# Gated mix of two attentions: half of the value units moved from the lead into the main steps, output units cut in two, differences reduced by relu in the lead

## The chip, the cores and the metric

The kernel runs on one core of a Trainium2 chip. The metric is device time in microseconds from the first to the last instruction of a launch, as the median of several runs. One execution was also recorded by the hardware profiler; all views below are of that execution. Engines: PE (matmul), DVE (vector), ACT (activation), POOL (GpSimd) and SP, which here only issues DMAs. Each engine works through its own instructions in order; semaphores order them against each other.

## The reference

Two attentions over the same x of 2048 positions and 576 features, 32 heads of 18 each. A has a key and a value for each head, B one key and one value for all heads. A sigmoid gate for each position mixes the two results:

```python
g = _sigmoid((x * gate_w).sum(-1, keepdims=True))
a = _A_ref(x, A_wqkv, A_wo)
b = _B_ref(x, B_wq, B_wk, B_wv, B_wo)
return g * a + (1 - g) * b
```

with, in each, softmax(q k^T / sqrt(18)) v for every head and an output matrix of 576 x 576. All is float32; the kernel splits numbers into a high and a low part to keep the precision.

## The kernel before, in words

**Heads and steps.** The 64 heads (`NU`; first the 32 of B, u < `H`, then the 32 of A) are worked off one after the other. A head has 16 steps, so there are 1024 (`NSTEP`). A step of the softmax takes 128 keys against all 2048 queries: four score matmuls of 512 columns (`step_scores`, L548), each followed by an exponential on ACT (L555) that writes a `pt` tile, and the output product (`step_pv`, L561), which multiplies the four `pt` tiles of an earlier step with the values and accumulates in the bank `acc`.

**The maxima.** The exponentials need the row maximum of each query. It is found `LEAD` = 22 steps ahead by `step_max`: for 128 queries, matmuls against the keys in four chunks of 512 (L511), each into a bank `pm`, and a reduction on DVE (L520). In the main steps one chunk of every second step is not reduced by itself. Instead the operation "x" multiplies with the difference of the keys of chunk 1 and chunk 0, ACT writes its relu to the tile `xb` (L514), and one custom DVE instruction (L517) adds `xb` to chunk 0 and takes the maximum, which covers both chunks. `max_rows` finishes a head's maxima; they go through DRAM into two extra rows of `qs`.

**Order.** The order of the work is written by hand, for two steps at a time (a pair, A and B), as strings at L789 to L795. "s" is a score, "m" a maximum (a capital M uses the other half of the PE rows), "x" the difference matmul for the next pair; P, Q, p, f, h, H are output products, whole (P, Q) or half; U takes one piece of the list `todo`; V projects values. The string of a plain pair and that of a pair with a unit:

```python
PLAIN = "sA0 mA2 sA1 mA0 sA2 mA3 P sA3 mB0 sB0 mB1 sB1 mB2 h sB2 mB3 sB3 x H"
UNIT = "sA0 mA2 sA1 mA0 sA2 mA3 P sA3 mB0 sB0 mB1 sB1 mB2 U sB2 mB3 sB3 x Q"
```

END stands for the last pair of a head (step number divisible by 16), AFTER for the one behind it. A score and the maximum next to it use different rows of the PE array and run at the same time.

**Banks.** The eight PSUM banks are three for scores (`ps_s`), four for maxima and for everything else that needs a bank for a short time (`ps_m`), and `acc`. A pool hands its banks out in turn; a matmul waits until the last reader of its bank is done.

**Stages.** First the projections of q and k for all heads (L240). Then the lead, steps -22 to -1: eleven pairs of maxima with no scores yet (`LEADS`), and between them 32 value units (`project_v`, L289): for one block of 128 positions and one half of A's heads 14 matmuls of 288 columns into a score bank, a copy on ACT (L292) and a store to DRAM, from where groups of four heads are loaded again later. Then the main steps. In steps 522 to 848 the first output segment (`out_proj` with `first`) adds 32 units of twelve matmuls (L677) and a copy on ACT (L683), in pairs with the string UNIT, one piece each (`at_ends`); the second segment follows in steps 942 to 1007 with a unit in nearly every pair, evicted by DVE. From step 1002 there are no more maxima (ALONE), and a short tail adds the last head.

Of the kernel before, what the change touches and what calls it, by code (L numbers as in the profile page):

```python
# [8 lines left out]
F32 = mybir.dt.float32  # L9
# [29 lines left out]


def q_row(u):
    return ROW_Q + DH * u if u < H else ROW_Q + DH * H + 2 * DH * (u - H)
# [7 lines left out]
def gated_mix_kernel(ctx: ExitStack, tc: tile.TileContext, xT, wall, wv, wo, out):  # L50
# [109 lines left out]
    def turn_mask():  # L160
        pt = ps_m.tile([P, 512], F32, name="pm")
# [31 lines left out]
    def balance(g):  # L193
# [9 lines left out]
        yield  # L203
        pt = ps_m.tile([P, 512], F32, name="pm")
        nc.tensor.transpose(pt[0:2, 0:P], r, ident)
# [5 lines left out]
        yield  # L211
        pb = ps_m.tile([P, 512], F32, name="pm")
        nc.tensor.matmul(pb[:, 0:2], two, dg, start=True, stop=True)
# [58 lines left out]
    def shared_v(c):  # L272
        st = ST.pop(c)
        pv = ps_m.tile([P, 512], F32, name="pm")
# [117 lines left out]
    vwp = ph1.enter_context(tc.tile_pool(name="vwp", bufs=1, side="right"))  # L392
    VS = [None, None]

# [3 lines left out]
    def project_rest():  # L398
        bal = None
        for n in range(12, len(JOBS)):  # L400
            mt, c = JOBS[n]
            if c == 0 and mt + 1 < MT:
                WP.append(prep_w(W[mt + 1]))
            project(n)
            for m in range(*AT.get(n, (0, 0))):
                measure_a(m, W[m])
            if n == 13:
                bal = balance(2)
            if n in (13, 14):
                next(bal)  # L410
            if n == 15:
                run(bal)
            if c == 0:
                if mt == 4:
                    load_k(ksb, ROW_KB, nc.gpsimd)
                    load_kd(kdb, ROW_KB, nc.gpsimd)
                if mt == 5:
                    load_q(0, nc.gpsimd)
                if mt in (6, 7):
                    load_q(mt - 5, nc.gpsimd)  # L420
                if mt in (7, 10):
                    hf = (mt - 7) // 3
# [45 lines left out]
    def open_ph2():  # L468
# [6 lines left out]
        L["kds"] = [p2.tile([P, 512], F16, name="kda"), kdb]  # L475
        L["oacc"] = p2.tile([P, 16, D], F32, name="oacc")
        for t in L["ks"][:2]:
# [13 lines left out]
    def v_of(u, kt):  # L491
# [3 lines left out]
        return VG[g][:, kt, 19 * i:19 * i + 19]  # L495

    MX = {}

    def step_max(u, i, c, low=False):

# [10 lines left out]
        nc.tensor.matmul(pm, qs[u % 3][b:b + 54, i * P:(i + 1) * P], k, start=True, stop=True)  # L511
# [135 lines left out]
    def out_proj(t0, rows, first=False):  # L647

        nt = len(rows)
        oacc = L["oacc"]  # L650
        O = {}
# [14 lines left out]
        for q in range(8):  # L666
# [3 lines left out]
            for s2 in range(2):  # L670
                st_ = 2 * q + s2
                for hf in range(2):
                    fp = ps_m.tile([P, 512], F32, name="pm")
                    n = 0
                    for a, b in PRODS:
                        for t, r in enumerate(rows):
                            nc.tensor.matmul(fp[:, 0:288], o[b][:r, t, s2 * P:(s2 + 1) * P],  # L677
                                             w[a][:r, t, 288 * hf:288 * hf + 288],
# [25 lines left out]
    def last_out():  # L704
# [6 lines left out]
        for j in range(4):  # L711
# [3 lines left out]
            dma(stk[36:54, cs], ol[32 * j:32 * j + 18, :])  # L715
        pt = ps_m.tile([P, 512], F32, name="pm")
        for c in range(4):
# [7 lines left out]
        for st_ in range(16):  # L725
            for hf in range(2):
                ps = ps_m.tile([P, 512], F32, name="pm")
                nc.tensor.matmul(ps[:, 0:288], stk[0:54, st_ * P:st_ * P + P],
# [41 lines left out]
    for t0, rows, Ta, Tb, Tc in SEG:  # L770
        when(Ta, lambda t0=t0, rows=rows: slow.append(prep_wo(t0, rows)))
        when(Tb - 4, lambda t0=t0, rows=rows: (todo.append(out_proj(t0, rows, first=t0 == 0)), pull(1)))
    when(980, lambda: slow.append(prep_last()))


    at_ends = list(range(528, 849, 16)) + list(range(522, 843, 32))
    assert len(at_ends) == 32

    def due(T, t0, t1, n):
        if t0 == SEG[0][3]:  # L780
            return at_ends.count(T)
# [12 lines left out]
    ALONE = "sA0 sA1 P U sA2 sA3 U sB0 sB1 h U sB2 sB3 H U"  # L794
    LEADS = "V.A mA0 MA1 mA2 MA3 V.B mB0 MB1 mB2 MB3"  # L795
    order = None
    for T in range(-LEAD, NSTEP + 2, 2):
# [8 lines left out]
        units = sum(due(t, Tb, Tc, 32) for t in (T, T + 1) for _, _, _, Tb, Tc in SEG)  # L806
        order = LEADS if T < 0 else FIRST if T == 0 else ALONE if alone else UNIT if units else \
            END if T % 16 == 0 else AFTER if order is END else PLAIN
        for op in order.split():
            k, second, c = op[0], op[1:2] == "B", op[2:]  # L810
            if k == "V":
                while len(vunits) > 32 * (-T - 1 - (c == "B")) // LEAD:
                    project_v(*vunits[0], WV[vunits[0][1]])
# [4 lines left out]
            elif k in "mM":  # L818
                step_max(*divmod(M + second, 16), int(c), k == "M")
            elif k == "s":  # L820
# [57 lines left out]
```

## Time and profile before

| what | value |
|---|---|
| median of 3 runs | 2726.04 us (2725.89 to 2726.05) |
| the profiled execution | 2726.16 us, span 2724.3 us |
| PE, DVE, ACT busy | 99%, 89%, 88% of the span |
| projections, before the lead | to 224.7 us |
| the lead | 224.7 us to 307.2 us (start of the first exponential) |
| the main steps, relu of step 0 to relu of step 998 | 312.6 us to 2637.7 us |

How to read the rows that follow. A row of the timeline or of the chain begins with its start and its duration in us, then engine, line, operation and tiles (output, arrow, inputs), shape, and the number of instructions that are merged in the row; in square brackets stands the idle time of the engine before it and who ended it. A row of the table by stage begins with the stage (from:to), then its length, then busy time and number of instructions for each engine named in its first row, then the granted PE clock, the share of the DMA engines and GB/s. Matmul records of neighbours overlap, so the distance between starts tells more than the durations. In the rows `pm` is a maxima bank, `ps` a score bank; `kdb` and `kda` as inputs mark the difference matmul x.

### The profile page before, as it was taken

Reading aid. Unit: us, or ns where it says so; the run is one execution under the profiler, and the core shown is the slowest. Engines: PE = TensorE matmul, PEld = TensorE weight load, DVE = VectorE, ACT = ScalarE, POOL = GpSimd, SP = SyncE. Lnnn points to the kernel's source line nnn. Section 1 sums busy time; section 2 is a strip of 40 time slices with the busy share of each in tenths; the row PEclk is TensorE's granted clock in tenths of the full one; section 3 lists DMA queues with packets and bytes.
Section 4 is the critical chain, followed back from the end, with each engine's and each line's share of the span. In section 5 each row is a group of like instructions: output and inputs, shape, how many; then the busy total and the mean of one; then the engine's idle time right before and its main releaser. Section 6 shows DMA issues by size and latency. Waiting matters only on the chain.

```text
span 2724.3 us, 57935 instructions
## 1 busy us (share of the span) xinstructions
PE 2689.0 (99%) x22210; PEld 957.2 (35%) x22210; DVE 2421.9 (89%) x4589; ACT 2389.5 (88%) x4809; POOL 285.7 (10%) x531
## 2 busy tenths in 40 slices
PE   8999999999999999999999999999999999999999
PEld 6767522222222222222222333333333332223444
DVE  6335899999999999999999999999999999998865
ACT  4332599999999999999999999999999999998875
POOL 3641000001000200110110001000100021001000
PEclk9999999999999999999999999999999999999998
DMA  6322100002001100110132113112221112122312
GB/s 188 114 97 85 38 16 19 20 22 59 27 18 32 45 26 17 45 43 20 32 72 80 41 49 97 40 41 57 72 66 48 47 58 64 39 68 85 89 36 95
DMA packets 127089, 150.36 MB, mean 55 GB/s; under 512 B 55339, under 2 KB 94411, under 8 KB 125614
## 3 DMA queue, kind: packets, MB, share of 16 engines
q1 hardware_dynamic: 113628, 121.86, 15.8%
q0 software_dynamic: 7968, 19.23, 2.1%
q10 hardware_dynamic: 5216, 5.57, 0.6%
q8 instruction: 174, 2.85, 0.4%
q14 instruction: 103, 0.84, 0.1%
HBM read 90.89 MB, written 46.45 MB: 50 GB/s over the span
## 4 chain that ended last, share of the span: by engine, by line
ACT 50%; PE 40%; DVE 6%; DMA 2%; issue 1%; SPq 1%; POOL 0%; DVEq 0%; ACTq 0%; POOLq 0%
ACT pt L555 45%; PE acc L561 13%; PE ps L548 11%; ACT xb L514 6%; PE pm L677 4%; PE ps L240 4%; PE pm L240 4%; DVE mx L520 3%; PE ps L289 3%; PE pm L511 1%; SPq L56 1%; DMA R<-r_d 1%; DVE oe L571 1%; DVE junk L517 1%; DVE oacc L731 0%
## 5 line engine op out<-in xcount | busy, mean ns | idle before, releaser
L555 ACT ACTIVATE pt<-ps 128x512 f32<-128x512 f32 x4052 | 2093.2, 637 | 67.8 <-PE pm L511 59.8
L520 DVE TENSOR_REDUCE mx<-pm 128x1 f32<-128x512 f32 x3096 | 1941.4, 683 | 93.6 <-PE pm L511 52.8
L548 PE MATMUL ps<-qs,ksb 56*128 56x512 f16 x2688 | 818.4, 380 | 10.7
L511 PE MATMUL pm<-ksb,qs 54*128 54x512 f16 x2364 | 742.2, 383 | 2.2 <-DVE mx L520 1.1
L561 PE MATMUL acc<-pt,vb 128*19 128x512 f32 (+1 forms) x6136 | 592.2, 458 | 1.9
L561 PE MATMUL acc<-pt,vg 128*19 128x256 f32 (+1 forms) x5664 | 579.5, 481 | 2.3 <-DVE oe L571 0.5
L511 PEld LDWEIGHTS <-qs 54*128 54x128 f16 x4096 | 332.2, 93 | 245.6 <-issue 196.7
L548 PE MATMUL ps<-qs,ksa 56*128 56x512 f16 x1364 | 404.3, 379 | 4.8 <-ACT pt L555 1.3
L548 PEld LDWEIGHTS <-ksb 56*128 56x128 f16 x2688 | 175.0, 94 | 622.1 <-issue 575.8
L511 PE MATMUL pm<-ksa,qs 54*128 54x512 f16 x1232 | 384.8, 382 | 0.5 <-ACT xb L514 0.2
L517 DVE CUSTOM_DVE_ANT_0 junk<-pm,xb 128x512 bf16<-128x512 f32 x500 | 340.6, 681 | 0.0
L514 ACT ACTIVATE xb<-pm 128x512 f32<-128x512 f32 x500 | 316.6, 633 | 0.0
L548 PEld LDWEIGHTS <-ksa 56*128 56x128 f16 x1408 | 89.3, 94 | 328.8 <-issue 298.1
L530 POOL TENSOR_SCALAR mt<-mt 128x32 f32<-128x32 f32 x64 | 18.6, 290 | 1612.0 <-DVE mt L528 1612.0
L561 PEld LDWEIGHTS acc<-pt,vb 128*19 128x19 f32 x6136 | 104.1, 96 | 223.5 <-issue 206.4
L561 PEld LDWEIGHTS acc<-pt,vg 128*19 128x19 f32 x5664 | 96.1, 97 | 222.8 <-issue 204.9
L511 PE MATMUL pm<-kdb,qs 54*128 54x512 f16 x372 | 141.5, 380 | 0.0
L248 ACT ACTIVATE ph<-ps,tv 128x512 f16<-128x512 f32 x29 | 19.8, 686 | 67.3 <-PE ps L240 43.2
L292 ACT ACTIVATE vst<-ps 128x288 f32<-128x288 f32 x32 | 13.2, 412 | 67.4 <-PE ps L289 67.4
L571 DVE COPY oe<-acc 128x512 f32<-128x512 f32 x63 | 43.6, 692 | 30.0 <-PE acc L561 27.9
L248 ACT ACTIVATE ph<-pm,tv 128x512 f16<-128x512 f32 x27 | 18.4, 686 | 54.5 <-PE pm L240 40.6
L254 DVE SCALAR_TENSOR_TENSOR pl<-pm,tv,ph 128x512 f16<-128x512 f32 x27 | 20.1, 749 | 48.8 <-ACT ph L248 38.7
(151 smaller groups left out, 1518.6 us busy)
## 6 DMA issues: line engine op xcount, KB each, us to landing
qs<-qkh SPq DMA_DIRECT2D x244, 72.0 KB
qs<-qkl SPq DMA_DIRECT2D x122, 72.0 KB
onh<-oh SPq DMA_DIRECT2D x32, 256.0 KB
onl<-ol SPq DMA_DIRECT2D x32, 256.0 KB
oih<-onh SPq DMA_DIRECT2D x16, 512.0 KB
oil<-onl SPq DMA_DIRECT2D x16, 512.0 KB
ot<-oe SPq DMA_DIRECT2D x220, 36.0 KB
R<-r_d SPq DMA_DIRECT2D x55, 144.0 KB
```

Of the source, the lines that this page charges most:

```text
L240: nc.tensor.matmul(fp[:, a0:b0], w[a][:kr, k, :], X[b][:kr, k, s0 + a0:s0 + b0], start=(n == 0), stop=(n == len(PROJ) - 1), skip_group_che ...
L248: nc.scalar.activation(h, fp, AF.Copy, scale=t)
L289: nc.tensor.matmul(fp[:, 0:288], X[b][:kr, k, st_ * P:(st_ + 1) * P], w[a][:kr, k, :], start=(n == 0), stop=(n == len(PROJ) - 1))
L511: nc.tensor.matmul(pm, qs[u % 3][b:b + 54, i * P:(i + 1) * P], k, start=True, stop=True)
L514: nc.scalar.activation(MX["x", u, i], pm, AF.Relu)
L517: nc.vector.tensor_tensor_reduce(junk, pm, MX.pop(("x", u, i)), 1.0, -3e38, op0=OP.add, op1=OP.max, accum_out=MX[u][:, i, c:c + 1])
L520: nc.vector.tensor_reduce(MX[u][:, i, c:c + 1], pm, axis=AX.X, op=OP.max)
L548: nc.tensor.matmul(ps, kst(u)[b:b + 56, i * P:(i + 1) * P], qs[u % 3][b:b + 56, c * 512:(c + 1) * 512], start=True, stop=True)
L555: nc.scalar.activation(pt, ps, AF.Exp, scale=SCALE / LIFT ** 2)
L561: nc.tensor.matmul(acc[32 * j:32 * j + 19, a:b], v_of(u, i), PT[u, i, j][:, a:b], start=(i == 0 and a == 0), stop=(i == 15), skip_group_ch ...
L571: nc.vector.tensor_copy(oe, acc)
L677: nc.tensor.matmul(fp[:, 0:288], o[b][:r, t, s2 * P:(s2 + 1) * P], w[a][:r, t, 288 * hf:288 * hf + 288], start=(n == 0), stop=(n == 3 * nt ...
```

## The change

Banks: `ps_m` shrinks from four to three; the fourth becomes a pool of its own, `ps_x`, whose bank `side()` hands out. Value units, output units, the transposes of the setup and every fourth of the banks asked for through `four()` use it. `four()` serves the maxima of the lead and the tail, the plain `ps_m` the maxima of the main steps.

Values: only the first half of A's heads (16 units) is projected in the lead. The other 16 units are made by the new `value_units` among steps 16 to 434, each in two bursts of seven matmuls in the place of U: positions and weights are loaded again from DRAM and split on GpSimd, two units share double buffers, and the tiles live where the output accumulator and the first output weights are later. Pairs with a burst take the string UNIT instead of PLAIN, END or AFTER.

Output: the first segment's 32 units are cut in two bursts of six, 64 pieces from step 524 on (`pieces`).

Lead: its first pair reduces all eight chunks and ends with an x; the other ten replace one reduction of step A by that relu, as the main steps do, and the first main pair has one maximum less.

```diff
+VPROD = PROJ[:-1] + [("l", "h", NKT - 1, 128)]
...
-    ps_m = ctx.enter_context(tc.tile_pool(name="ps_m", bufs=4, space=PSUM))
+    ps_m = ctx.enter_context(tc.tile_pool(name="ps_m", bufs=3, space=PSUM))
+    ps_x = ctx.enter_context(tc.tile_pool(name="ps_x", bufs=1, space=PSUM))
...
+    turn = {"n": 0}
+
+    def side():
+        return ps_x.tile([P, 512], F32, name="px")
+
+    def four():
+
+        turn["n"] += 1
+        return side() if turn["n"] % 4 == 0 else ps_m.tile([P, 512], F32, name="pm")
...
-                if mt in (9, 12):
-                    hf = (mt - 9) // 3
-                    WV.append({y: vwp.tile([P, NKT, 288], F32R, name=f"vw{y}{hf}") for y in "hl"})
-                    split_w(VS[hf], WV[hf], nc.vector)
+                if mt == 9:
+                    WV.append({y: vwp.tile([P, NKT, 288], F32R, name=f"vw{y}") for y in "hl"})
+                    split_w(VS[0], WV[0], nc.vector)
...
+    def value_units():
...
+        def parts(src, st, h, l):
+            dma(st[:, 0:4, :], src[0:512, :].rearrange("(k p) m -> p k m", p=P))
+            for b in (0, 64):
+                dma(st[b:b + 64, 4, :], src[512:576, :])
+            return st, h, l
...
+        def cut(st, h, l):
+            split(st, h, l, nc.gpsimd, nc.gpsimd)
+            return {"h": h, "l": l}
...
+        for st_ in range(16):
+
+            nc.gpsimd.tensor_tensor(x["h"][64:128, 4], st[64:128, 4], x["h"][64:128, 4].bitcast(F32), op=OP.subtract)
+            if st_ < 15:
+                nxt = positions(st_ + 1)
+            yield
+            fp = side()
+            for n, (a, b, k, kr) in enumerate(VPROD):
+                if n == 7:
+                    yield
+                nc.tensor.matmul(fp[:, 0:288], x[b][:kr, k, :], w[a][:kr, k, :],
+                                 start=(n == 0), stop=(n == len(VPROD) - 1))
+            t = vs[st_ % 2]
+            nc.scalar.activation(t[:, :, 0:18], fp[:, 0:288].rearrange("p (h d) -> p h d", d=18), AF.Copy)
+            dma(v_d[st_, :, 304:608], t.rearrange("p h d -> p (h d)"))
+            if st_ < 15:
+                x = cut(*nxt)
+                st, h, l = nxt
...
-        pm = ps_m.tile([P, 512], F32, name="pm")
+        pm = four() if lead_on else ps_m.tile([P, 512], F32, name="pm")
...
-                    fp = ps_m.tile([P, 512], F32, name="pm")
+                    fp = four() if "tail" in L else side()
                     n = 0
                     for a, b in PRODS:
                         for t, r in enumerate(rows):
+                            if first and n == 6:
+                                yield
...
+    when(0, lambda: (todo.append(value_units()), pull(1)))
...
-    at_ends = list(range(528, 849, 16)) + list(range(522, 843, 32))
-    assert len(at_ends) == 32
+    pieces = [524 + 11 * i // 4 * 2 for i in range(64)]
+
+    vpieces = [0] + [16 + 27 * i // 4 * 2 for i in range(32)]
...
-    vunits = [(st_, hf) for hf in range(2) for st_ in range(16)]
+    vunits = [(st_, 0) for st_ in range(16)]
...
-    FIRST = "sA0 mA2 sA1 mA0 sA2 mA3 mA1 sA3 mB0 sB0 mB1 sB1 mB2 sB2 mB3 sB3 x"
+    FIRST = "sA0 mA2 sA1 mA0 sA2 mA3 sA3 mB0 sB0 mB1 sB1 mB2 sB2 mB3 sB3 x"
...
-    LEADS = "V.A mA0 MA1 mA2 MA3 V.B mB0 MB1 mB2 MB3"
+    LEAD0 = "V.A mA0 MA1 mA2 MA3 V.B mB0 MB1 mB2 MB3 x"
+    LEADS = "V.A mA2 MA0 mA3 V.B mB0 MB1 mB2 MB3 x"
...
+        if T >= NSTEP - 6:
+            L["tail"] = True
```

More of the change, by code (lines that the diff above doesn't have):

```diff
@@ L160, in turn_mask @@
     def turn_mask():
-        pt = ps_m.tile([P, 512], F32, name="pm")
+        pt = side()
         for g in range(4):
@@ L203, in balance @@
         yield
-        pt = ps_m.tile([P, 512], F32, name="pm")
+        pt = side()
         nc.tensor.transpose(pt[0:2, 0:P], r, ident)
@@ L211, in balance @@
         yield
-        pb = ps_m.tile([P, 512], F32, name="pm")
+        pb = side()
         nc.tensor.matmul(pb[:, 0:2], two, dg, start=True, stop=True)
@@ L273, in shared_v @@
         st = ST.pop(c)
-        pv = ps_m.tile([P, 512], F32, name="pm")
+        pv = side()
         for j in range(4):
@@ L392, in gated_mix_kernel @@
     vwp = ph1.enter_context(tc.tile_pool(name="vwp", bufs=1, side="right"))
-    VS = [None, None]
+    VS = [None]
     for b in (SB, MB):
@@ L475, in open_ph2 @@
         L["kds"] = [p2.tile([P, 512], F16, name="kda"), kdb]
-        L["oacc"] = p2.tile([P, 16, D], F32, name="oacc")
         for t in L["ks"][:2]:
@@ L495, in v_of, with place, positions, step_max @@
         return VG[g][:, kt, 19 * i:19 * i + 19]
+    def value_units():
+        rooms = {"r": (F32R, "oacc"), "w": (F32, "woh4"), "x": (F32, "wol4")}
+        used = {"r": 0, "w": 0, "x": 0}
+        room = {r: L["pool"].tile([P, 16 * D if r == "r" else 4 * D], t, name=f"room_{r}", tag=g)
+                for r, (t, g) in rooms.items()}
+        def place(r, k, m):
+            n = used[r]
+            used[r] += k * m
+            return room[r][:, n:n + k * m].rearrange("p (k m) -> p k m", m=m)
+        def parts(src, st, h, l):
[3 more added lines that the diff above has]
+            return st, h, l
+        XV = [[place(r, NKT, P) for r in "xrr"] for j in range(2)]
+        def positions(st_):
+            return parts(xT[:, P * st_:P * st_ + P], *XV[st_ % 2])
+        def cut(st, h, l):
+            split(st, h, l, nc.gpsimd, nc.gpsimd)
+            return {"h": h, "l": l}
+        nxt = positions(0)
+        w = parts(wv[:, 288:576], *[place(r, NKT, 288) for r in "wrr"])
+        vs = [place("x", 16, 19) for i in range(2)]
+        yield
+        w = cut(*w)
+        x = cut(*nxt)
+        st, h, l = nxt
+        for t in vs:
+            nc.gpsimd.memset(t, 1.0)
+        for st_ in range(16):
[13 more added lines that the diff above has]
+            if st_ < 15:
+                x = cut(*nxt)
+                st, h, l = nxt
     MX = {}
-    def step_max(u, i, c, low=False):
+    def step_max(u, i, c, low=False, lead_on=False):
         if u not in MX:
@@ L649, in out_proj @@
         nt = len(rows)
+        if first:
+            L["oacc"] = L["pool"].tile([P, 16, D], F32, name="oacc")
         oacc = L["oacc"]
@@ L676, in out_proj @@
                         for t, r in enumerate(rows):
+                            if first and n == 6:
+                                yield
                             nc.tensor.matmul(fp[:, 0:288], o[b][:r, t, s2 * P:(s2 + 1) * P],
@@ L715, in last_out @@
             dma(stk[36:54, cs], ol[32 * j:32 * j + 18, :])
-        pt = ps_m.tile([P, 512], F32, name="pm")
+        pt = four()
         for c in range(4):
@@ L726, in last_out @@
             for hf in range(2):
-                ps = ps_m.tile([P, 512], F32, name="pm")
+                ps = four()
                 nc.tensor.matmul(ps[:, 0:288], stk[0:54, st_ * P:st_ * P + P],
@@ L805, in gated_mix_kernel @@
         alone = M >= NSTEP
-        units = sum(due(t, Tb, Tc, 32) for t in (T, T + 1) for _, _, _, Tb, Tc in SEG)
-        order = LEADS if T < 0 else FIRST if T == 0 else ALONE if alone else UNIT if units else \
+        units = sum(due(t, Tb, Tc, 32) for t in (T, T + 1) for _, _, _, Tb, Tc in SEG) + vpieces.count(T)
+        order = LEAD0 if T == -LEAD else LEADS if T < 0 else FIRST if T == 0 else ALONE if alone else UNIT if units else \
             END if T % 16 == 0 else AFTER if order is END else PLAIN
@@ L818, in gated_mix_kernel @@
             elif k in "mM":
-                step_max(*divmod(M + second, 16), int(c), k == "M")
+                step_max(*divmod(M + second, 16), int(c), k == "M", T < 0)
             elif k == "s":
```

8 lines of the change are left out of this document (4 added, 4 removed).

## The prediction

> **What bounds the kernel now.** I read the busy time of each engine by stage first, then the chain of waits in the lead, then the timelines of single pairs of steps.
>
> ```profile
> span 2724.3 us, 57935 instructions
> ...
> core 0: us, PE busy (x) PEld busy (x) DVE busy (x) ACT busy (x) POOL busy (x), PEclk, DMA share, GB/s
> 224.70:307.20 82.50, 82.35 (x540) 65.13 (x540) 54.27 (x90) 14.19 (x35) 2.78 (x13) 1.00 0.20 70
> 349.40:1355.50 1006.10, 995.95 (x8964) 281.40 (x8960) 987.08 (x1881) 994.07 (x2017) 65.91 (x129) 1.00 0.11 30
> ```
>
> The stage that the change empties, the lead (224.7 to 307.2 us), has PE full and ACT nearly idle. The main stage has PE, DVE and ACT all at 98 or 99%, but a busy matmul time says little about PE there (records overlap), so the stages must be read instruction by instruction. The lead, in the chain of waits:
>
> ```profile
> 224.75 4.49 PE ps L289 x28
> 229.24 0.45 PE pm L511 x3
> 229.69 2.26 PE ps L289 x14
> 231.94 0.45 PE pm L511 x3
> ```
>
> Each value unit (14 matmuls) holds PE 2.25 us, each four maxima 0.45 us, with nothing between them. DVE waits for PE there: four reductions take 2.48 us, 0.62 each, and the next four matmuls come 2.7 us after the last at the earliest (229.24 to 231.94).
>
> ```profile
> 229.38 2.48 DVE L520 TENSOR_REDUCE mx<-pm 128x1 f32<-128x512 f32 x4 [3.07 <-PE ps L289]
> ```
>
> Now one pair of the main stage. The string PLAIN orders it: A0, A1, A2 are scores and maxima of the first step, then P, an output product, then A3 and the second step.
>
> ```profile
> 687.14 0.60 ACT L555 ACTIVATE pt<-ps 128x512 f32<-128x512 f32 x1
> ...
> 687.33 0.39 PE L511 MATMUL pm<-ksb,qs 54*128 54x512 f16 x1
> 687.55 0.38 PE L511 MATMUL pm<-ksb,qs 54*128 54x512 f16 x1
> 687.62 0.61 ACT L514 ACTIVATE xb<-pm 128x512 f32<-128x512 f32 x1
> 687.80 0.39 PE L511 MATMUL pm<-ksb,qs 54*128 54x512 f16 x1
> 688.10 4.06 ACT L555 ACTIVATE pt<-ps 128x512 f32<-128x512 f32 x8
> 688.12 1.06 PE L561 MATMUL acc<-pt,vb 128*19 128x512 f32 x8
> ...
> 689.11 0.39 PE L548 MATMUL ps<-qs,ksb 56*128 56x512 f16 x1
> ...
> 690.08 0.63 PE L561 MATMUL acc<-pt,vb 128*19 128x256 f32 x8
> 690.64 0.39 PE L548 MATMUL ps<-qs,ksb 56*128 56x512 f16 x1
> ...
> 692.03 0.61 ACT L514 ACTIVATE xb<-pm 128x512 f32<-128x512 f32 x1
> ```
>
> From relu to relu 4.41 us: nine ACT instructions, 0.48 us apart at the relu (687.62 to 688.10) and 0.49 behind it ((4.06 - 0.60) / 7). But P sits on this path as well: it starts at 688.12, and the score behind it (sA3) starts only at 689.11, 0.99 us later. ACT comes to sA3's exponential after three others, at 688.10 + 3 x 0.48 to 0.49 = 689.54 to 689.57, which is 0.43 to 0.46 us after that score's start. Where ACT stands idle and waits for this score (the next fence), the delay is 0.42. So sA3 arrives just in time, with hardly any slack. The half product h at 690.08 holds PE 0.56.
>
> **The change, part by part.**
>
> *Three banks for the maxima instead of four.* This is the largest term. The difference matmul of one pair (x) is followed by mA2, mA0 and mA3 of the next. At 687.80, when mA3 starts, x is held by its relu until 687.62 + 0.61 = 688.23, mA2 by its reduction, and mA0 by the custom instruction, which reads the relu's result. With four banks there is one left. With three there is none, and x's is the first to come free. So mA3 waits until 688.28 (an exponential's bank, released at 687.14 + 0.60 = 687.74, was taken by sA2 beside mA3 at 687.80: 0.05 to see a release), 0.48 late; P is queued behind it on PE, sA3 behind P, and ACT waits for sA3. The new loop is relu 0.61, release 0.05, mA3 to P 0.31 (687.80 to 688.12), P 0.99, sA3 to ACT 0.42, then A3, B0 to B3 up to the next relu, 5 x 0.48 = 2.40: 4.78 us where 4.41 stood. The trace has one pair where exactly this happens, because DVE was late and mA3's bank with it:
>
> ```profile
> 870.28 0.37 PE L511 MATMUL pm<-kdb,qs 54*128 54x512 f16 x1
> ...
> 871.35 0.61 ACT L514 ACTIVATE xb<-pm 128x512 f32<-128x512 f32 x1
> ...
> 872.08 0.37 PE L511 MATMUL pm<-ksb,qs 54*128 54x512 f16 x1
> 872.38 1.05 PE L561 MATMUL acc<-pt,vb 128*19 128x512 f32 x8
> ...
> 873.37 0.39 PE L548 MATMUL ps<-qs,ksb 56*128 56x512 f16 x1
> ...
> 873.79 2.56 ACT L555 ACTIVATE pt<-ps 128x512 f32<-128x512 f32 x5 [0.36 <-PE pm L511]
> ...
> 876.19 0.64 ACT L514 ACTIVATE xb<-pm 128x512 f32<-128x512 f32 x1
> ```
>
> mA3 started 0.12 us after the relu's end, ACT stood idle 0.36 us, and the pair took 4.84 us. Less 0.07 for the later start, that is my 4.78.
>
> The pair at a head's end (END) has the same chain up to A3 and then three steps to its relu: 2.38 + 1.44 = 3.82, now 3.36:
>
> ```profile
> 669.56 0.61 ACT L514 ACTIVATE xb<-pm 128x512 f32<-128x512 f32 x1
> ...
> 672.92 0.69 ACT L514 ACTIVATE xb<-pm 128x512 f32<-128x512 f32 x1
> ```
>
> How many pairs, and what they take on average now (the relus counted by stage):
>
> ```profile
> core 0: us, ACT busy (x), PEclk, DMA share, GB/s
> 349.40:1355.50 1006.10, 143.79 (x224) 1.00 0.11 30
> 1503.10:2262.80 759.70, 99.69 (x160) 1.00 0.20 56
> 2480.20:2620.00 139.80, 14.48 (x24) 1.00 0.26 79
> ```
>
> A plain pair is 1006.1 / 224 = 4.49 us, eight to a head of 16 steps. Of the eight, five are as above and lengthen by 0.33 (4.78 against 4.41 to 4.49); END adds 0.46. Of the two after END, x comes early in one, so that nothing is late (taken as 0), and in the other mA3 waits for the last maximum of the pair before: taken as 0.25, between 0 and 0.43. Sum 2.4 us for a head. Bounds: 1.6 if only the five change, 3.4 if all eight lose the 0.43 of the late pair. Steps 4 to 942 are 58.6 heads: +141 (94 to 199). The last stage (24 pairs in 139.8, 5.82 each) is bound by PE's unit of twelve matmuls in every pair; the relu is done there before mA3. +3 (0 to 7) for some 30 pairs.
>
> *The lead.* 16 units leave: 16 x 2.25 = 36 us off PE. What remains on PE is 16 x 2.25 + 22 x 0.45 = 46 us. DVE has 8 + 10 x 7 = 78 reductions at 0.62, 48 us, now the longer. The two alternate: five pairs hold two units, 5.4 us on PE; six hold one, 4.3 on DVE; 53 in all, from 48 if the banks smooth it to 58 if each unit delays DVE. The relu of the differences lies on an ACT that is 17% busy. From 82.5 to 53: -29 (-34 to -24). The second half's weight split, no longer done in the projections, lay beside a full PE: nothing.
>
> *Value units in the main stage.* Thirty-two bursts of seven matmuls, in place of h (half an output product). Costs from the unit of twelve that the output projection has now, and its copy:
>
> ```profile
> 1803.34 0.39 PE L511 MATMUL pm<-ksa,qs 54*128 54x512 f16 x1
> 1803.65 0.80 PE L677 MATMUL pm<-woh,oih 128*128 128x288 f32 x4
> ...
> 1805.45 0.39 PE L548 MATMUL ps<-qs,ksa 56*128 56x512 f16 x1
> 1805.56 0.41 ACT L683 ACTIVATE oacc<-pm 128x288 f32<-128x288 f32 x1 [0.81 <-PE pm L677]
> ```
>
> Twelve matmuls hold PE 1.80 us, 0.15 each; seven 1.05 to 1.1, six 0.9 to 0.95. Against h's 0.56 us a burst of seven puts the next score (sB2) 0.5 late, of which ACT's queue hides 0.1: +0.4, and +0.1 for the whole product (0.99) that then comes after x in place of a half. The second burst brings ACT the copy as well, 0.41: together +0.75. 16 x 1.25 = +20 (10 to 30). GpSimd's splits and SP's loads are issued a unit, some 30 us, ahead; behind SP's wait for the copy stand only the loads of q and of the row maxima, which have pairs to spare.
>
> *Output units in bursts of six.* A unit costs now (759.7 - 160 x 4.49) / 30 = 1.37 us, with 30 of the 32 units in that window; 32 make 44. In two bursts: 0.3 + 0.1 and, with the copy, 0.55, 0.95 a unit, 30 in all: -13 (-20 to -5). The tail's bank rotation is the same four: nothing.
>
> Sum on the profiled execution's own 2726.16 (span 2724.3): -29 + 141 + 3 + 20 - 13 = +122, so 2848. The median of the runs, 2726.04, is the same to 0.1, and I forecast **2848**.
>
> **The rivals.**
>
> *The bank is not missed* (not slower, faster even). If sA3's exponential had 0.48 us or more to spare, the late mA3 would cost nothing: 2726 - 29 + 20 - 13 = 2704. For it: DVE is busy only 7 x 0.6 of 4.49 us in a pair, and PE 3.9 (0.99 and twice 0.56 for the output products, eight times 0.22, as 687.33 to 687.55, for the scores with the maxima beside them). Against it: the 0.42 us from sA3 to ACT in every plain pair. It decides from there: below 0.48 of slack the pair lengthens. Chance 0.08.
>
> *DVE binds too.* If late banks also hold mB1 and mB2, all eight pairs lose the 0.43 of the late pair, 3.4 a head: 2848 + 58 = 2906. For it: at 870 to 876 two pairs in a row were long. Against it: a longer pair gives DVE 0.3 us more for the same seven reductions. Chance 0.08.
>
> *PE is throttled.* Waits for a bank leave PE idle more often. One stretch at half clock stands in the trace, where the order of the first steps waited for DVE:
>
> ```profile
> 310.20:317.10 6.90, 6.83 (x27) 1.10 (x26) 5.72 (x11) 4.68 (x9) 0.00 (x0) 0.51 0.00 0
> ...
> 312.58 0.60 ACT L514 ACTIVATE xb<-pm 128x512 f32<-128x512 f32 x1
> ...
> 319.22 0.60 ACT L514 ACTIVATE xb<-pm 128x512 f32<-128x512 f32 x1
> ```
>
> It made a pair of 4.49 last 6.64, 2.15 more. Once a head: 58.6 x 2.15 = +126, 2974. Against it: PE would still work 3.9 of 4.78 us, and the late pair at 872 kept its clock. Chance 0.03. The Trainium skill speaks for this rival ("TensorE: Matmul & The Clock Gate", "A second HAM failure mode: psum-queue depth-cycling"): micro-idles of PE between groups of matmuls that cycle through PSUM banks made its clock swing between half and full. The 1006 us above, with full clock, do not show it with four banks.
>
> *The lead stays long* (relu or DVE hold it near 72): 2867, inside the range; chance 0.05.
>
> **How the numbers follow.** Forecast 0.74, 2704 with 0.08, 2906 with 0.08, 2974 with 0.03, 2867 with 0.05; 0.02 is left for an outcome within 0.2% of before, about what a measurement of this kernel can tell from no change. All lower bounds together (94, -34, 10, -20, 0) give 2776, all upper ones 2936; not all fall to one side, so 2785 to 2912, which takes in the second rival and leaves out the first. Faster 0.08, same 0.02, slower 0.90.
>
> **What would show it.** Right: relu to relu 4.75 to 4.85 us in plain pairs, mA3 starting about 0.05 us after the relu's end, ACT with an idle gap of 0.3 us or more in each pair before A3's exponential, ACT's share of the main stage near 92%; first exponential 24 to 34 us earlier; a unit's two bursts about 0.95 us together over plain pairs. Wrong: pairs still at 4.41 (first rival), DVE without gaps in longer pairs (second), a clock below 1.00 in the main stage (third).

## The result, and the profile after

The changed kernel takes 2864.3 us (median of 4 runs, 2862.8 to 2866.3), the kernel before 2726.0 (4 runs, 2724.9 to 2726.1) on the same chip: ratio 1.0509, 95% interval 1.0491 to 1.0527. It is slower by 138 us; the forecast was 2848, the range 2785 to 2912. The profiled execution has a span of 2862.9 us against 2724.3, so 138.6 us are to be found. Of the runs further below, one execution of the kernel with whole units took 3365.8 us at a granted clock of 0.667, and its ratio leaves that one out.

First the pages of the two profiles: the chain that ended last by engine, and the exponentials' row (behind the second bar: ACT's idle time just before them, and what ended most of it). Before:

```profile
ACT 50%; PE 40%; DVE 6%; DMA 2%; issue 1%; SPq 1%; POOL 0%; DVEq 0%; ACTq 0%; POOLq 0%
...
L555 ACT ACTIVATE pt<-ps 128x512 f32<-128x512 f32 x4052 | 2093.2, 637 | 67.8 <-PE pm L511 59.8
```

After:

```profile
PE 88%; issue 4%; POOL 3%; DVE 3%; ACT 2%; POOLq 0%; DVEq 0%; ACTq 0%
...
L623 ACT ACTIVATE pt<-ps 128x512 f32<-128x512 f32 x4052 | 2133.7, 619 | 195.1 <-PE pm L579 186.3
```

The same 4052 exponentials now wait 195.1 us where they waited 67.8, nearly always until a maximum's matmul has run (the score beside it on the other rows of the array is what ACT needs). ACT has left the chain and PE has taken its place. The reader should not read that as "PE is the bound": in the main steps PE waits too, as the pair below shows.

The stages after, in the same table as before: the lead (first value matmul to first exponential), a stretch of it, steps 16 to 464, and the last stage. The columns are the stage and its length, then busy time with the number of instructions on PE, PEld, DVE, ACT and POOL, the granted clock, and two columns on DMA.

```profile
core 0: us, PE busy (x) PEld busy (x) DVE busy (x) ACT busy (x) POOL busy (x), PEclk, DMA share, GB/s
228.49:292.99 64.50, 54.91 (x315) 36.63 (x315) 48.80 (x91) 13.95 (x30) 2.78 (x13) 0.95 0.18 57
239.50:246.30 6.80, 6.13 (x23) 4.78 (x23) 3.33 (x8) 1.01 (x2) 0.00 (x0) 0.50 0.04 14
337.87:1430.25 1092.38, 1085.22 (x8891) 260.87 (x8889) 1006.32 (x1878) 1022.99 (x2032) 106.06 (x174) 1.00 0.12 34
...
2630.80:2776.16 145.36, 145.36 (x1060) 58.35 (x1056) 117.26 (x225) 112.19 (x218) 8.20 (x15) 1.00 0.23 68
```

The lead shrank from 82.5 to 64.5 us. The 224 pairs of the third row took 1006.1 us before and now 1092.4, with ACT busy 93.6% of it in place of 98.8%, and a full clock. The 24 pairs of the last row went from 139.8 to 145.4.

Cut at the relus of both traces, the 138.6 us are: setup up to the lead +3.8 (224.7 to 228.5), lead -18.0, first exponential to relu of step 0 -0.9, steps 0 to 442 +86.0, 442 to 522 +11.3, 522 to 872 +38.8, 872 to 942 +10.8, 942 to 998 +6.6, the rest +0.2.

A plain pair after, in the timeline (start, duration, engine, line, operation):

```profile
1407.16 0.64 ACT L582 ACTIVATE xb<-pm 128x512 f32<-128x512 f32 x1
...
1407.85 0.37 PE L579 MATMUL pm<-ksb,qs 54*128 54x512 f16 x1
1408.15 1.05 PE L629 MATMUL acc<-pt,vb 128*19 128x512 f32 x8
1409.14 0.39 PE L616 MATMUL ps<-qs,ksb 56*128 56x512 f16 x1
...
1409.56 2.56 ACT L623 ACTIVATE pt<-ps 128x512 f32<-128x512 f32 x5 [0.29 <-PE pm L579]
...
1411.97 0.64 ACT L582 ACTIVATE xb<-pm 128x512 f32<-128x512 f32 x1
```

This is the forecast loop: the relu ends at 1407.80, mA3 starts 0.05 later, P 0.30 behind it, sA3 0.99 behind P, ACT 0.42 behind sA3, and the next relu 2.41 later. Together 4.81 us, where 4.41 stood. A head without any unit in it is 38.43 us long where it was 35.86. From the relus of both traces: its five plain pairs take 4.81 for 4.41 to 4.54, the END pair 3.86 for 3.36, the two pairs behind END 3.40 for 3.40 and 7.13 for 6.86.

### The profile page after: what moved, and what is told of

Same layout as the page of the kernel before. It is cut to its first block, busy times and chain, and to the rows that moved or that the text cites. A ratio compares the mean times of both kernels' runs of the same rounds, so it can differ in the third digit from the quotient of the medians.

```text
span 2862.9 us, 56879 instructions
## 1 busy us (share of the span) xinstructions
PE 2823.1 (99%) x21602; PEld 857.9 (30%) x21602; DVE 2447.9 (86%) x4587; ACT 2436.6 (85%) x4817; POOL 333.5 (12%) x583
## 4 chain that ended last, share of the span: by engine, by line
PE 88%; issue 4%; POOL 3%; DVE 3%; ACT 2%; POOLq 0%; DVEq 0%; ACTq 0%
PE acc L629 36%; PE ps L616 33%; PE pm L579 10%; PE px L749 4%; ACT pt L623 1%; PE px L556 1%; DVE mx L588 1%; PE ps L303 1%; POOL qkh L59 1%; POOL qkl L59 1%; PE ps L254 1%; DVE oacc L803 0%; PE pm L254 0%; POOL wl L150 0%; ACT xb L582 0%
## 5 line engine op out<-in xcount | busy, mean ns | idle before, releaser
L623 ACT ACTIVATE pt<-ps 128x512 f32<-128x512 f32 x4052 | 2133.7, 619 | 195.1 <-PE pm L579 186.3
L579 PE MATMUL pm<-ksb,qs 54*128 54x512 f16 x2334 | 762.1, 380 | 11.9 <-DVE mx L588 2.1
L616 PE MATMUL ps<-qs,ksb 56*128 56x512 f16 x2688 | 762.6, 380 | 0.8
L629 PE MATMUL acc<-pt,vb 128*19 128x256 f32 (+1 forms) x5848 | 585.0, 472 | 0.0
L629 PE MATMUL acc<-pt,vg 128*19 128x512 f32 (+1 forms) x5344 | 571.4, 499 | 0.4 <-DVE oe L639 0.4
L579 PE MATMUL pm<-ksa,qs 54*128 54x512 f16 x1232 | 400.4, 379 | 3.4 <-ACT xb L582 0.4
L616 PE MATMUL ps<-qs,ksa 56*128 56x512 f16 x1364 | 381.4, 380 | 0.6
L579 PEld LDWEIGHTS <-qs 54*128 54x128 f16 x4096 | 290.0, 94 | 59.5 <-issue 29.6
L262 ACT ACTIVATE ph<-pm,tv 128x512 f16<-128x512 f32 x27 | 18.4, 686 | 54.5 <-PE pm L254 40.6
L268 DVE SCALAR_TENSOR_TENSOR pl<-ps,tv,ph 128x512 f16<-128x512 f32 x29 | 21.6, 748 | 46.2 <-ACT ph L262 26.3
```

The source lines that it names most:

```text
L262: nc.scalar.activation(h, fp, AF.Copy, scale=t)
L268: nc.vector.scalar_tensor_tensor(l, fp, t, h, op0=OP.mult, op1=OP.subtract)
L616: nc.tensor.matmul(ps, kst(u)[b:b + 56, i * P:(i + 1) * P], qs[u % 3][b:b + 56, c * 512:(c + 1) * 512], start=True, stop=True)
L623: nc.scalar.activation(pt, ps, AF.Exp, scale=SCALE / LIFT ** 2)
L629: nc.tensor.matmul(acc[32 * j:32 * j + 19, a:b], v_of(u, i), PT[u, i, j][:, a:b], start=(i == 0 and a == 0), stop=(i == 15), skip_group_ch ...
```

## Experiments

The theory at the start: the fourth bank alone makes the main stage's loss. The rivals: the open units, the bursts, or DVE. Where a run has one time only, the kernel before ran beside it (2725.1 to 2725.7).

**Three banks and nothing else.** The kernel before; whole output units and the setup's transposes use the fourth bank, value units and lead stay.

```diff
-    ps_m = ctx.enter_context(tc.tile_pool(name="ps_m", bufs=4, space=PSUM))
+    ps_m = ctx.enter_context(tc.tile_pool(name="ps_m", bufs=3, space=PSUM))
+    ps_x = ctx.enter_context(tc.tile_pool(name="ps_x", bufs=1, space=PSUM))
...
-                    fp = ps_m.tile([P, 512], F32, name="pm")
+                    fp = ps_x.tile([P, 512], F32, name="px")
```

> The kernel before with one edit: three banks for the maxima instead of four, the fourth used for the transposes of the setup and for whole output units. No value unit is moved, no unit is cut, the lead is the old one. Theory (the bank sets the pair: mA3 waits for the relu, P and sA3 behind it): plain pairs 4.8 us from relu to relu, a plain head 38.4 instead of 35.9, in all 2870 to 2895 us, and some 4 us more in the setup, where the transposes then share one bank. Rival (the main steps are longer because of the moved value units, their loads and GpSimd's splits): at most 2740 us, pairs at 4.41.

Measured 2932.91 us, above what was expected, but for reasons outside the main steps. Its timeline:

```profile
1440.97 0.65 ACT L515 ACTIVATE xb<-pm 128x512 f32<-128x512 f32 x1
...
1443.38 2.56 ACT L556 ACTIVATE pt<-ps 128x512 f32<-128x512 f32 x5 [0.29 <-PE pm L512]
1445.78 0.65 ACT L515 ACTIVATE xb<-pm 128x512 f32<-128x512 f32 x1
```

The pair is 4.81 us and the plain head 38.43, to the hundredth those of the changed kernel, with no unit cut and none moved. So the loss of the main steps is the bank's. The excess lies on both sides of them. The relu of step 0 comes 20 us later than before (332.8 against 312.6): the lead has three banks for its maxima and takes 98.5 us for 82.5, and it starts 4 us later, since the setup's transposes share one bank. The part behind step 998 takes 33 us longer, since there every output unit goes through the one side bank: near the end the units follow each other 1.64 us apart, each waiting until DVE has emptied that bank. The granted clock is 0.50 there over the last 45.6 us, where before it was so over 14.5; how much of the 33 us is the clock's was not separated. In the changed kernel, whose lead and tail take every fourth bank from the side through `four()`, the part behind step 998 is as long as before (86.8 us against 86.6).

**The bank given back.** The changed kernel with one pool of four; an open unit holds one of them.

```diff
-    ps_m = ctx.enter_context(tc.tile_pool(name="ps_m", bufs=3, space=PSUM))
-    ps_x = ctx.enter_context(tc.tile_pool(name="ps_x", bufs=1, space=PSUM))
+    ps_m = ctx.enter_context(tc.tile_pool(name="ps_m", bufs=4, space=PSUM))
...
-        return ps_x.tile([P, 512], F32, name="px")
+        return ps_m.tile([P, 512], F32, name="pm")
```

> The changed kernel with four banks in one pool again, from which the units take theirs too; a cut unit then holds one of the four from its first to its second burst. Theory: 35.9 us a head where no unit is open (steps 434 to 524 and 870 to 942), 38.4 or so while one is open, which is about half the time elsewhere; in all 2755 to 2800 us. Rival (not the banks): no change, about 2864 us.

Measured 2777.07, in the middle. Two heads in the table of relus (stage and length, ACT's busy time and number of relus, clock, DMA):

```profile
core 0: us, ACT busy (x), PEclk, DMA share, GB/s
1353.15:1389.00 35.85, 5.15 (x8) 1.00 0.16 44
897.85:938.40 40.55, 5.13 (x8) 1.00 0.14 43
```

(The stages are cut just inside the relus.) The first has no unit open and takes what it took before, 35.86 from relu to relu. The second has a value unit open from its first pair to its last, so three banks are left: its plain pairs are 4.81 again, and the head with both bursts takes 40.6, as in the changed kernel. What costs is not which pool the fourth bank is in, but that it is out of the maxima's turn while a unit is open, and a burst unit is open for two to seven pairs.

**Three attempts to take one step out of the loop.** If the loop relu, mA3, P, sA3 sets the pair, then x earlier, P ahead of mA3, or half of P behind sA3 should each break it. All three keep three banks and change only the order strings.

```diff
# x earlier
-    PLAIN = "sA0 mA2 sA1 mA0 sA2 mA3 P sA3 mB0 sB0 mB1 sB1 mB2 h sB2 mB3 sB3 x H"
+    PLAIN = "sA0 mA2 sA1 mA0 sA2 mA3 P sA3 mB0 sB0 mB1 sB1 x h sB2 mB2 sB3 mB3 H"
# P ahead of mA3
+    PLAIN = "sA0 mA2 sA1 mA0 sA2 P mA3 sA3 mB0 sB0 mB1 sB1 mB2 h sB2 mB3 sB3 x H"
# P in halves
+    PLAIN = "sA0 mA2 sA1 mA0 sA2 mA3 p sA3 mB0 f sB0 mB1 sB1 mB2 h sB2 mB3 sB3 x H"
```

UNIT is changed likewise in each, END in the last two.

> The changed kernel with x moved ahead of h or U in the strings PLAIN and UNIT (x h sB2 mB2 sB3 mB3), so that its relu runs after sB1's exponential and its bank is free long before mA3. Still three banks. Theory: the pair falls back to 4.41 to 4.55 us, a plain head to 35.9 to 36.5, in all 2715 to 2760 us. Rival (three banks are too few for DVE whatever the order): pairs over 4.65 us, over 2800 us.

> The changed kernel with P moved ahead of mA3 (in END ahead of mB0), so that the output product is no longer queued behind the waiting maximum. The bank wait itself stays. Theory: P covers the wait, pairs 4.45 to 4.6 us, in all 2735 to 2790 us. Rival (the wait for the bank costs what it costs, wherever P stands): pairs near 4.8 us, about 2864 us.

> The changed kernel, three banks, with the whole product P cut into its halves p and f in PLAIN, UNIT and END: p stays where P was, f follows after mB0 (in END mB1). Between mA3 and sA3 then stand 0.56 us of PE in place of 0.99. Theory (the loop relu, bank, mA3, product, sA3, exponential): pair 4.81 - 0.43 = 4.38, bounded by ACT and DVE at 4.41 to 4.55; in all 2715 to 2770 us. Rival (three banks starve DVE, the product's length does not matter): 4.8 us, about 2864 us.

Measured 2870.26, 2995.27 and 2916.25: three misses, the last two slower even than their rivals had it. Each broke the loop that it aimed at, and each pair came out longer than the 4.81 it started from. The timelines show a wait for each that accounts for it. With x earlier (a pair of 4.83):

```profile
1418.18 2.59 ACT L623 ACTIVATE pt<-ps 128x512 f32<-128x512 f32 x5
...
1419.35 0.37 PE L616 MATMUL ps<-qs,ksb 56*128 56x512 f16 x1
1419.67 1.05 PE L629 MATMUL acc<-pt,vb 128*19 128x512 f32 x8
1420.66 0.39 PE L616 MATMUL ps<-qs,ksb 56*128 56x512 f16 x1
...
1421.09 1.57 ACT L623 ACTIVATE pt<-ps 128x512 f32<-128x512 f32 x3 [0.31 <-PE pm L579]
```

mA3 no longer waits for the relu. But the relu now runs ahead of the exponentials B2 and B3, and sA2 needs one of the three score banks, the one that B3's exponential reads until about 1419.30 (the second of the five from 1418.18). So sA2 starts at 1419.35, P 0.32 behind it, sA3 0.99 behind P, ACT 0.42 behind that: 1.79 us from B3's end, which A0, A1 and A2 cover with 3 x 0.49. The gap of 0.3 is back, now from the score banks: the time is the rival's, the cause is not DVE.

With P ahead of mA3 (a pair of 4.96):

```profile
1463.68 3.08 DVE L588 TENSOR_REDUCE mx<-pm 128x1 f32<-128x512 f32 x5
1464.42 0.37 PE L579 MATMUL pm<-ksb,qs 54*128 54x512 f16 x1 [0.21 <-DVE mx L588]
...
1465.29 0.39 PE L616 MATMUL ps<-qs,ksb 56*128 56x512 f16 x1
...
1465.71 1.08 ACT L623 ACTIVATE pt<-ps 128x512 f32<-128x512 f32 x2 [0.42 <-PE pm L579]
```

sA3 is on time, but mA3 comes behind P, DVE gets it late (1463.68), and mB2 waits until DVE has reduced mA3 out of its bank. The half product h and the score sB2 stand behind mB2, and ACT waits 0.42 for that score: the same three banks, through DVE.

With P in halves (a pair of 4.89):

```profile
1423.82 0.60 ACT L582 ACTIVATE xb<-pm 128x512 f32<-128x512 f32 x1
...
1424.47 0.37 PE L579 MATMUL pm<-ksb,qs 54*128 54x512 f16 x1
...
1426.22 0.39 PE L616 MATMUL ps<-qs,ksb 56*128 56x512 f16 x1
...
1426.64 2.18 ACT L623 ACTIVATE pt<-ps 128x512 f32<-128x512 f32 x4 [0.26 <-PE pm L579]
```

sA3 now comes in time, and the next score, sB0, does not: two halves of 0.56 lie between mA3 and it, 1.75 us in all. Relu 0.60, release 0.05, 1.75, then 0.42 to ACT and four exponentials up to the next relu (2.07) make 4.89.

**The same cut in the kernel before.** The question left by that miss: is P with four banks a limit already, or is PE?

> The kernel before, four banks, with the same cut of P. Theory (there too the product stands on the path, from a score bank's release through sA2, P and sA3 to the exponential, which ties with ACT's nine instructions): pairs 4.30 to 4.41 us, in all 2680 to 2726 us. Rival (ACT alone sets 4.41, and the second half product only costs PE 0.13 more): 2726 to 2745 us.

Measured 2764.41, 39 us slower than before and slower than either expectation, with plain pairs of 4.52. PE in such a pair:

```profile
688.56 0.63 PE L561 MATMUL acc<-pt,vb 128*19 128x256 f32 x8
...
689.48 0.63 PE L561 MATMUL acc<-pt,vb 128*19 128x256 f32 x8
...
693.01 0.63 PE L561 MATMUL acc<-pt,vb 128*19 128x256 f32 x8
```

The rows are p, f and the next pair's p; h and H lie between the last two. In the 4.45 us from p to p the trace shows no stop of PE: a score with its maximum every 0.22 to 0.33 us, 0.56 to 0.59 for each of the four halves. The cut itself costs PE 0.2 us (2 x 0.56 in place of 0.99, and 0.31 ahead of one more product where 0.22 stood). PE therefore has about 4.2 us of work in an uncut pair of 4.41, and not the 3.9 that the first rival of the prediction was argued with. With 0.2 us to spare, PE cannot make up for a maximum that comes 0.48 late, and a cut of P uses that slack up by itself.

**x early in the lead.** The changed kernel, with x ahead of the maxima, and the setup's transposes of the values taken from `ps_m`.

```diff
-    LEADS = "V.A mA2 MA0 mA3 V.B mB0 MB1 mB2 MB3 x"
+    LEADS = "V.A x mA2 MA0 mA3 V.B mB0 MB1 mB2 MB3"
...
-        pv = side()
+        pv = ps_m.tile([P, 512], F32, name="pm")
```

> The changed kernel with two edits ahead of the main steps: x stands right behind the first value unit of a lead pair instead of at its end, and the transposes of the shared value take a maxima bank instead of the single side bank. Theory: the lead falls from 64.5 to 52 to 58 us (x at the end waits for DVE's banks and holds up the next value unit), and it starts near 224.7 instead of 228.5; in all 2850 to 2858 us. Rival (the lead is the sum of PE's and DVE's work, in whatever order): 64 us, 2860 or more.

Measured 2862.12, no change in the whole, yet the stages moved. The lead of this kernel:

```profile
core 0: us, PE busy (x) PEld busy (x) DVE busy (x) ACT busy (x) POOL busy (x), PEclk, DMA share, GB/s
230.50:287.20 56.70, 50.32 (x317) 34.74 (x317) 47.89 (x90) 14.16 (x31) 2.77 (x13) 1.00 0.18 61
```

56.7 us for 64.5, and at full clock. But it starts 2.0 us later: out of three `ps_m` banks the transposes wait longer than out of the side bank (the first start at 43.66 where they started at 35.62), a miss of that half. From the first exponential on 3 us are given back. So the place of x explains 8 of the 11 us by which the lead fell short of the forecast, the half clock that comes with it included, and the setup's loss is not cured by another pool of three. With one pool of four the same holds: the lead takes 62.7 us with x at its end (the run with the bank given back) and 56.6 with x early (the next run).

**Four banks, whole units.** With the order of the last run for the lead, one pool of four, value units in one burst of fourteen at steps 16 + 26i, output units whole at the old places.

```diff
-                if n == 7:
-                    yield
...
-                            if first and n == 6:
-                                yield
...
-    vpieces = [0] + [16 + 27 * i // 4 * 2 for i in range(32)]
+    vpieces = [0] + [16 + 26 * i for i in range(16)]
```

> The changed kernel with four banks in one pool, value units whole (14 matmuls, 16 bursts among steps 16 to 406), output units whole and placed as before, and the lead's order as in the run above. No bank is held over pairs. Theory: plain pairs 4.41 again, lead 52 to 58 us, a value unit some 1.6 us, so -27 + 16 x 1.6 = -1 against the kernel before: 2715 to 2735 us. Rival (moving the units costs more than their bursts, through loads, GpSimd or DVE): over 2745 us.

Measured 2726.95, and in a second, longer comparison:

> The kernel of 2726.95 (four banks, all 16 value units whole) once more, timed against before: ratio 0.999 to 1.002. It tells whether moving all sixteen with the bank kept is a gain, a loss or nothing.

2727.36 (11 runs) against 2725.38 (27 runs), ratio 1.0008, interval 0.9999 to 1.0017. All of the loss is gone, and so is all of the gain. A pair with a value unit:

```profile
498.39 0.65 ACT L579 ACTIVATE xb<-pm 128x512 f32<-128x512 f32 x1
...
500.88 2.12 PE L553 MATMUL pm<-room_r 128*128 128x288 f32 x14
...
503.03 0.41 ACT L556 ACTIVATE room_x<-pm 128x288 f32<-128x288 f32 x1 [1.06 <-PE pm L553]
...
504.32 0.60 ACT L579 ACTIVATE xb<-pm 128x512 f32<-128x512 f32 x1
```

5.93 us for the pair, and 4.69 for the one behind it. From the relu of step 0 to that of step 434 the kernel before takes 974.7 us, this one 1002.3: 1.72 us for each of the 16 units. Up to the relu of step 0 it is 27.2 ahead (285.4 against 312.6), 1.70 for each unit. The two cancel.

**Only some of the units moved.** If the lead's gain is not linear, fewer units should do better: as long as PE sets the lead, each unit that leaves gives its full 2.25 us. The edit is shown against the run above; the loops over the units change with it.

```diff
-    vpieces = [0] + [16 + 26 * i for i in range(16)]
+    vpieces = [0] + [16 + 52 * i for i in range(8)]
...
-    vunits = [(st_, 0) for st_ in range(16)]
+    vunits = [(st_, 0) for st_ in range(16)] + [(st_, 1) for st_ in range(8)]
```

> Four banks, whole value units as in the kernel of 2726.95, but only 8 of the 32 units leave the lead (steps 16 + 52i), 24 stay there. There a unit cost the main stage 27.6 / 16 = 1.72 us, and the lead and setup gave 27.2 / 16 = 1.70 back, so all was lost again. Theory: the lead's gain isn't linear: as long as PE sets it, each unit gives its full 2.25 us, and only the last ones give little, since DVE's 48 us of reductions then set the lead. So 8 units give 18 and cost 14: 2719 to 2723. Rival: PE and DVE alternate in the lead from the first unit on and each gives 1.7: no change, 2725 to 2728.

> The same with 12 units moved (steps 16 + 36i), 20 left in the lead (20 x 2.25 + 10 = 55 us of PE beside 48 of DVE). Theory: gain 24 to 27, cost 12 x 1.72 = 20.6: 2719 to 2724, near the kernel with 8. Rival (linear): 2725 to 2728.

Measured with 8 units 2719.95 (11 runs), ratio to before 0.9980, interval 0.9971 to 0.9989; with 12 units 2722.27, 0.9989, interval 0.9980 to 0.9998. Both as the theory had it. The stages with 8 units, the lead and steps 0 to 434:

```profile
224.19:289.19 65.00, 64.22 (x428) 48.99 (x429) 48.43 (x90) 17.45 (x39) 2.77 (x13) 1.00 0.21 69
293.97:1282.09 988.12, 978.48 (x8707) 284.34 (x8706) 955.75 (x1818) 965.36 (x1958) 85.35 (x148) 1.00 0.12 33
```

and the lead with 16:

```profile
224.00:280.60 56.60, 51.12 (x317) 34.89 (x317) 47.90 (x90) 14.18 (x31) 2.77 (x13) 1.00 0.19 62
```

The first eight units take 17.5 us out of the lead (82.5 to 65.0), 2.2 each, and PE is still full there. The second eight take 8.4, 1.05 each, and neither PE (51.1) nor DVE (47.9) is full. In the main steps a unit costs 1.68 ((988.1 - 974.7) / 8). So the first eight gain and the others lose. With eight units moved the kernel is the fastest found, 5 us (0.2%) ahead of the kernel before.

## Why the prediction held, point by point

The mechanism was right and decided the sign: a maxima bank less makes mA3 wait for the relu, P and sA3 stand behind it, and ACT waits for sA3. The run with three banks alone shows it, the run with four takes it away. The terms, in us:

| term | forecast | after |
|---|---|---|
| setup | 0 | +3.8 |
| lead, with the first pair | -29 | -18.9 |
| three banks, steps 0 to 942 | +141 | +149 |
| value bursts | +20 | +15 |
| output units in halves | -13 | -17 |
| last stage | +3 | +6.6 |
| sum | +122 | +138.6 |

The two rows of bursts are what is left of steps 0 to 442 and 522 to 872 after 2.57 us for each head (27.6 heads, 71.0 of 86.0; 21.9 heads, 56.2 of 38.8). The total came out nearer than its terms: setup, lead, banks and last stage cost 25 us more than forecast, the two kinds of bursts 9 us less. That these partly cancel is luck.

*Three banks.* Forecast 4.78, 3.82 and +0.25 for the plain pair, END and the second follower; measured 4.81, 3.86 and +0.26. A head is 2.57 longer, not 2.4, mostly because its five plain pairs started from 4.45 on average and gain 0.36 each, not 0.33; the 4.49 that the prediction calls a plain pair is the mean of all pairs, END and its followers included.

*The lead* was the mis-sized term. "53 in all" took PE and DVE to alternate without loss; it took 64.5. The place of x at the end of the lead's order was overlooked: it waits for a bank that DVE frees, and the next value unit stands behind it.

```profile
237.01 0.38 PE L579 MATMUL px<-ksb,qs 54*128 54x512 f16 x1
237.02 0.69 DVE L588 TENSOR_REDUCE mx<-pm 128x1 f32<-128x512 f32 x1 [0.96 <-PE ps L303]
...
240.17 0.58 PE L579 MATMUL pm<-kdb,qs 54*128 54x512 f16 x1 [0.82 <-DVE mx L588]
...
244.78 0.69 DVE L588 TENSOR_REDUCE mx<-px 128x1 f32<-128x512 f32 x1 [3.46 <-PE px L579]
```

DVE stands idle while PE works off the unit behind x, PE while DVE reduces, and here PE fell to half clock as well (0.50 in the stretch 239.5 to 246.3). With x early the lead takes 56.7, inside the forecast's -34 to -24; the last 3 us to the forecast of 53 are not explained. In the changed kernel itself one of the named signs fails by this: the first exponential comes 14.2 us earlier, not 24 to 34.

*Setup.* Costed at nothing, in effect, since `side()` was not followed into it. The second transposes of the setup wait 2.56 us for the copy out of the only side bank:

```profile
45.40 0.22 DVE L293 COPY vb<-px 128x72 f32<-128x72 f32 x1
45.77 0.58 PE L290 MATMUL px<-ident,pst 18*128 18x18 f32 x4 [2.56 <-DVE vb L293]
```

Most of the 3.8 us is not the wait itself. In this execution the granted clock stands at 0.50 from 45.0 to 51.8 us as well, beside a first such stretch from 34.7 to 41.6 that the kernel before has too (37.2 to 44.0). The run with P in halves has the same setup and such a wait (2.88) but no second stretch, and its lead starts at 226.0 in place of 228.5; the run with P ahead of mA3, with a second stretch of 3.4 us, starts it at 227.8. So some 2.5 of the 3.8 us go with the clock.

*Last stage.* "The relu is done there before mA3" holds to 0.08 us (mA3 starts at 2691.95, its neighbour sA2 at 2691.87). What was missed is the next turn of the three banks: mB2 needs the bank that DVE frees when it has reduced mA3 (the first of four reductions from 2693.10), and comes 0.15 later than its neighbours' spacing of 0.22; the unit stands behind it.

```profile
2693.10 2.49 DVE L588 TENSOR_REDUCE mx<-pm 128x1 f32<-128x512 f32 x4
...
2693.47 0.38 PE L579 MATMUL pm<-ksa,qs 54*128 54x512 f16 x1
2693.84 0.37 PE L579 MATMUL pm<-ksa,qs 54*128 54x512 f16 x1
```

The two delays make up a pair of 6.02 us for 5.80.

*Bursts.* Both were cheaper: a value unit 0.94 us in its two bursts, not 1.25 (15 us for 16), an output unit about 0.84 (1.37 less 17 / 32), not 0.95. A plain pair with a value unit's burst, the first or the second, takes 5.24 to 5.34 us (once 5.59), where 4.81 stands without. The second holds the copy of 0.41 as well and costs hardly more, so nearly all of that copy falls into time in which ACT would have waited; the forecast had added it in full.

*The rivals.* Bank not missed: false in every plain pair. DVE binds too: not in these orders, but one change of order away (P ahead of mA3, 2995). PE throttled in the main steps: no, the granted clock of steps 16 to 464 is 1.00, although PE waits for a bank in every pair. The Trainium skill ("TensorE: Matmul & The Clock Gate", "A second HAM failure mode: psum-queue depth-cycling") tells of a kernel whose clock swung with such waits; the main steps here do not show it. The lead stays long: half so, 64.5 lies between the forecast's 53 and this rival's 72.

*Slips in the working.* All upper bounds together give 2933, not 2936. The half clock at 310.2 is not the only one in the trace of before: 37.2 to 44.0 and the last 14.5 us have 0.50 too. PE's 3.9 us in a pair are about 4.2, as the cut of P showed. None of them moves the forecast.

What stays open: what makes up the 3 us that the run with x early gave back behind its lead, and whether a hand-made order for three banks could reach 4.41; the three tried did not. A part of the 3 us is the clock: at the first exponentials it stood at 0.50 for 10.2 us in that run and for 6.8 in the changed kernel, and two executions of the kernel with whole units that differ in the same way (6.8 and 10.2 us) differ by 1.0 us in steps 0 to 434.

## What to carry to other kernels

Before a buffer is taken out of a rotation, follow the in-order engine that waits for it: what stands behind the waiting instruction, and which engine's slack pays. In a loop where ACT's work (4.41 us), PE's (about 4.2) and the chain of waits (4.81) lie this close, an edit that breaks the one you see uncovers the next, so price all of them before the order is changed. And cost moved work by its marginal price at both ends: eight units moved gained 5 us, sixteen nothing.

## What the runs showed of the hardware that was not expected

PE's clock fell to half without a long stop. In the changed kernel's lead:

```profile
237.00:238.00 1.00, 0.61 (x4) 0.09 (x1) 0.98 (x2) 0.40 (x1) 0.00 (x0) 1.00 0.00 0
238.00:239.00 1.00, 0.54 (x3) 0.12 (x2) 1.00 (x4) 0.00 (x0) 0.00 (x0) 1.00 0.43 156
...
239.40:239.80 0.40, 0.00 (x0) 0.00 (x0) 0.40 (x2) 0.00 (x0) 0.00 (x0) 0.65 0.00 0
```

PE had a little over half a load in the two microseconds ahead of the drop at about 239.5, and the longest single gap in them was 0.39 us. The clock came back some 6.8 us later. The Trainium skill ("TensorE: Matmul & The Clock Gate", "What's actually happening") has the clock fall after at least one idle window of about 3.4 us. Taken as an unbroken idle time the trace does not agree: over the 3.41 us ahead of the drop PE was busy 2.39.

In the main steps PE waits in every pair (mA3 starts 0.42 us behind sA2, at 1407.85 and 1407.43, where scores in a row follow each other by 0.21 to 0.23) and keeps its full clock. How much load holds the clock was not measured.

The clock's stretches come in steps. Every stretch at half clock that ended before its kernel did, in all thirteen traces, lasted 3.4, 6.8, 10.2 or 13.7 us. The same code ran with different numbers of them: the setup with two (the changed kernel) and with one (P in halves), the kernel with whole units with 6.8 us at its first exponentials and with 10.2.
